# State products of a chunked scan in tiles of four heads instead of two, with a fourth output buffer and a new plan

## The chip, the cores and the metric

The kernel runs on one core of one Trainium2 chip. The metric is the device time of one execution in microseconds (us); lower is better. Before the change the median of three runs is 358.34 us (357.5 to 358.92).

## What is computed

A chunked state-space scan over `x` (4 batches, 8 heads, 768 steps, 32 channels, state size 16), whose result is the input of a gated feed-forward layer. All is float32. Cut to what matters:

```python
for c in range(nc):                       # the kernel uses chunks of 128 steps, in two halves of 64
    M = (C_c @ B_c.T) * L                 # L: decays between two steps, causal
    y_intra = M @ x_c
    y_inter = (C_c @ state) * exp(cum)    # what the state from before contributes
    y[c] = y_intra + y_inter
    state = decay_full * state + sum_j B_j x_j * decay_from_j     # 16 x 32 per head
x2 = y.transpose(0, 2, 1, 3).reshape(3072, 256)
out = (sigmoid(x2 @ w_gate) * (x2 @ w_val)) @ w_out               # 256 -> 1536 -> 256
```

## The kernel before, in words

The 768 steps are six chunks of 128 (`NCH`), and each chunk is two halves of 64 steps (`L2`). For each chunk the scan makes 512 token rows of the layer's input (four batches of 128), and the feed-forward part of chunk k (`gate`, `value`, `proj`) runs on the tensor engine (PE) while the scan of chunk k+1 is made. Chunk 0 has its own code (`FirstUnit`, one batch at a time); chunks 1 to 5 use class `Scan`. A float32 product that must keep full precision is either three products of float32r parts (L842, L871 to L873) or one plain f32 product (L518, L549, L564, L574, L867).

PE visits the scan of each chunk twice, between products of the feed-forward part. **Visit A** (`scan`) holds the products C·B (`multiply`, L549) and the halves' own state products (`own`, L574). **Visit B** (`weigh`) holds the weighted products (`within`, L564) and the products of C with the two states at the start of the two halves (L518). The states of the eight heads stand on 128 partitions, 16 rows a head.

`own` multiplies B (decayed, `bd`) by x for two heads at a time: a tile of 64 steps by 32 state rows (2 heads x 16) on PE, 64 columns of x (2 heads x 32) streamed through it. Half of what comes out belongs to the wrong head, so `chosen` (L582) multiplies it by a 0/1 mask on the vector engine (DVE). L518 uses such a state tile as weights, 32 rows by 64 columns, for 64 columns of C. Both make 32 products in a chunk (16 in `own` of chunk 5, which needs no state at its end), and each f32 product leaves two records in the trace.

The rest of the state: `early` (GpSimd, POOL) fades the old state by the decay of the first half (`sp`, L466), DVE adds the first half's own product (`sm`, L500), POOL fades that again (L466) and adds the second half's (L541) into `sn`.

The order of each engine is fixed in the program by a planner: every step has an engine, a cost, needs, and a due time (`DUES`); `VISIT_A` and `VISIT_B` are its costs for the two visits, `TURN` says behind which third of a projection visit B stands. PSUM gives the products three banks (`ps_mm`). Of the other functions the change touches, `proj` turns a projection by DVE transposes (L878) into `o` buffers, three in all, from which SyncE's queue (SP) writes the output (L885).

Of the kernel before, what the change touches and what calls it, by code (L numbers as in the profile page):

```python
# [44 lines left out]
}  # L45
WARM = (4, 4, 3)
# [12 lines left out]
POOL_SB = 1.32  # L59
# [15 lines left out]
VISIT_A, VISIT_B = 2.1, 2.68  # L75
HELD = 1
TURN = {2: 2, 3: 1, 4: 0, 5: 0}
# [8 lines left out]
def tile_ssd_then_gated_ffn(  # L86
# [21 lines left out]
    NG = H // NQ  # L108
    NK = DM // P
# [41 lines left out]
    nc.vector.tensor_reduce(of_h, eye.rearrange("p (h n) -> p h n", n=N), axis=mybir.AxisListType.X, op=ALU.add)  # L151
    of_g = const.tile([P, NG], F32, name="of_g")
# [7 lines left out]
    nc.gpsimd.tensor_copy(mask, of_g.rearrange("p (g o) -> p g o", o=1).broadcast_to([P, NG, D]))  # L160

# [46 lines left out]
    def run():  # L208
# [9 lines left out]
        spare = {"y": [0.0], "banks": [0.0] * 3, "cb": [0.0], "g": [0.0] * 3, "o": [0.0] * 3}  # L218
# [183 lines left out]
    def state_of(c, name, bufs):  # L402

        if (name, c) not in got:
            got[name, c] = wk.tile([P, NB, NG * D], F32, tag=name, name=f"{name}{c}", bufs=bufs)
        return got[name, c]
# [4 lines left out]
    class Scan:  # L411
# [51 lines left out]
        def faded(self, state, i):  # L463

            t = wk.tile([P, NB, NG * D], F32, tag="sp", name=f"sp{self.c}", bufs=1)
            nc.gpsimd.tensor_tensor(  # L466
                out=t, in0=state,
                in1=got["pp", self.c][:, :, i * L2 + L2 - 1 : (i + 1) * L2].broadcast_to([P, NB, NG * D]), op=ALU.mult,
            )
            return t  # L470

        def early(self):

            c = self.c
            yield step("pool", 0.7, [("S", c - 1)] + [("p", c, b) for b in range(NB)], [("sp", c)], port=True)
            self.sp = self.faded(states[c - 1], 0)

        def scan(self):

            c, more = self.c, self.more  # L480
            needs = [("mult", 0, b) for b in range(NB)] if c == 1 else []
            yield step(
                "pe", VISIT_A, [("bt", c), ("cg", c), ("xn", c), ("bdec", c)] + needs, [("cb", c)], cb=1, y=1, **({"banks": 1} if more else {})
            )
# [3 lines left out]
            pl = [pool.tile([P, NB, L2], F32, tag=tag, name=f"pl{c}") for pool, tag in ((ps_y, "py"), (ps_mm, "mm"))[: 1 + more]]  # L488
            for b in range(NB):
                own(self.bd[:, b], got["xn", c][:, b], lambda i, rows: pl[i][rows, b], b == 0, more)  # L490
            if more:
                yield step("dve", 0.42, [], [("after", c)], banks=-1)
                self.after = wk.tile([P, NB, NG * D], F32, tag="mr", name=f"mr{c}", bufs=1)
                chosen(self.after, pl[1], NB)
            yield step("dve", 0.42, y=-1)
            ml = wk.tile([P, NB, NG * D], F32, tag="ml", name=f"ml{c}", bufs=1)
            chosen(ml, pl[0], NB)
            yield step("dve", 0.42, [("sp", c)], [("first", c)], port=True)
            self.s1 = state_of(c, "sm", 1)
            nc.vector.tensor_tensor(out=self.s1, in0=self.sp, in1=ml, op=ALU.add)  # L500

        def weigh(self):
# [7 lines left out]
            yield step("pe", VISIT_B, [("mult", c), ("cd", c), ("first", c)] + ([("po", c - 1, 0, TURN[c])] if c > 1 else []), [("y", c), ("inter", c)])  # L510
# [58 lines left out]
    def own(bd, xn, out, first=False, more=True):  # L569

        for q in range(NQ):
            for i in range(2 if more else 1):
                half = slice(i * L2, (i + 1) * L2)
                nc.tensor.matmul(  # L574
                    out(i, slice(32 * q, 32 * q + 32)), bd[half, NG * q : NG * q + NG].rearrange("p g n -> p (g n)"),
                    xn[half, NG * q : NG * q + NG].rearrange("p g d -> p (g d)"),
                    start=first, stop=True, skip_group_check=True,
                )

    def chosen(out, local, n):  # L580

        nc.vector.tensor_tensor(  # L582
            out=out, in0=local,
            in1=mask.rearrange("p (o g) d -> p o (g d)", o=1).broadcast_to([P, n, NG * D]), op=ALU.mult,
        )

    class FirstUnit:
# [44 lines left out]
        def before(self):  # L632
# [3 lines left out]
            if ("cd", 0) not in got:  # L636
                got["cd", 0] = wk.tile([P, NB, L2], F32, tag="ml", name="cd0", bufs=1)
# [14 lines left out]
        def result(self):  # L652
# [35 lines left out]
            if ("mr", 0) not in got:  # L688
                got["mr", 0] = wk.tile([P, NB, NG * D], F32, tag="mr", name="mr0", bufs=1)
            self.after = got["mr", 0][:, b]  # L690
# [415 lines left out]
```

## Time and profile before

| | us |
|---|---|
| median of 3 runs | 358.34 |
| the profiled execution's own time | 358.31 |
| its span, first to last instruction | 356.2 |
| PE busy in it | 348.9 (98%) |
| DVE, ACT, POOL busy | 155.8, 134.2, 158.7 |

The profile is of one execution; 2.1 us of its time lie outside the span. "PEld" is the loading of weights into PE, which can overlap with its products; a wait is put down to what ended it. The chain of waits follows back from the last instruction to what released each step.

### The profile page before, as it was taken

The numbers are of one execution on the slowest core, as the hardware profiler recorded it, in microseconds if no ns is written. First come the engines' busy times: TensorE is split into PE (matmuls) and PEld (weight loads), VectorE is DVE, ScalarE is ACT, GpSimd is POOL, SyncE is SP. The second block draws the span as 40 slices with busy tenths as digits, with TensorE's granted clock in tenths as the row PEclk, the third lists the DMA queues.
The fourth block names the chain that finished last, engine by engine and source line by source line (L and its number), as shares of the span: only waits on it lengthen the run. The fifth ranks groups of instructions, "written<-read, shape, count | busy, mean of one in ns | idle before, by whom it ended". The sixth has DMA issues, their size and how long they took to land.

```text
span 356.2 us, 7756 instructions
## 1 busy us (share of the span) xinstructions
PE 348.9 (98%) x3174; PEld 269.8 (76%) x3174; DVE 155.8 (44%) x275; ACT 134.2 (38%) x241; POOL 158.7 (45%) x146
## 2 busy tenths in 40 slices
PE   8999999999999999999999999999999999999996
PEld 3674477457788888888888888888888888888885
DVE  6966677762474501655301655310655310232201
ACT  2667289242744401543410443320443320344400
POOL 4656377397698720357410357410365410244500
PEclk9999999999999999999999999999999999999999
DMA  6987999738644505445137321041200001200000
GB/s 130 194 249 249 265 210 216 133 65 60 99 93 90 81 19 72 89 93 72 32 44 137 50 46 25 29 63 25 33 4 2 1 4 25 33 4 0 1 31 29
DMA packets 96790, 27.57 MB, mean 77 GB/s; under 512 B 88370, under 2 KB 91442, under 8 KB 96114
## 3 DMA queue, kind: packets, MB, share of 16 engines
q1 hardware_dynamic: 96754, 27.07, 39.2%
q8 instruction: 25, 0.41, 0.5%
q14 instruction: 11, 0.09, 0.1%
HBM read 23.71 MB, written 3.34 MB: 76 GB/s over the span
## 4 chain that ended last, share of the span: by engine, by line
PE 81%; SPq 8%; DMA 7%; DVE 2%; issue 1%; DVEq 0%
PE pg L842 24%; PE pv L842 24%; PE po L871 6%; PE po L873 6%; PE po L872 6%; PE po L867 4%; DMA bq<-in_B_dram 3%; SPq L305 3%; PE po L908 2%; DMA wr<-in_moe_w_gate_dram 2%; SPq L342 2%; DMA wr<-in_moe_w_val_dram 2%; PE pcb L549 2%; PE pcb L564 2%; SPq L885 1%; PE pcb L518 1%
## 5 line engine op out<-in xcount | busy, mean ns | idle before, releaser
L801 POOL TENSOR_TENSOR h<-g,h 128x512 fp32r<-128x512 f32 x62 | 84.8, 1369 | 139.1 <-ACT h L799 139.1
L842 PE MATMUL pg<-xh,w 128*128 128x512 f32 x264 | 92.8, 392 | 1.3 <-DVE h L791 0.8
L842 PE MATMUL pv<-xh,w 128*128 128x512 f32 x264 | 92.1, 390 | 0.0
L795 DVE TENSOR_TENSOR g<-pv,g 128x512 f32<-128x512 f32 x62 | 42.8, 690 | 83.3 <-PE pv L842 82.9
L771 ACT ACTIVATE g<-pg 128x512 f32<-128x512 f32 x72 | 43.2, 600 | 68.6 <-PE pg L842 63.5
L799 ACT CAST h<-g 128x512 fp32r<-128x512 f32 x62 | 38.5, 620 | 78.8 <-DVE g L795 78.6
L842 PEld LDWEIGHTS pg<-xh,w 128*128 128x128 f32 x264 | 49.5, 188 | 13.4 <-DVE h L791 2.1
L842 PEld LDWEIGHTS pv<-xh,w 128*128 128x128 f32 x264 | 49.5, 188 | 10.6 <-POOL w L386 0.3
L842 PE MATMUL pg<-xl,w 128*128 128x512 f32 x132 | 51.4, 390 | 0.0
L842 PE MATMUL pv<-xl,w 128*128 128x512 f32 x132 | 51.4, 389 | 0.0
L871 PE MATMUL po<-h,w 128*128 128x512 f32 x100 | 40.2, 402 | 0.0
L873 PE MATMUL po<-h,w 128*128 128x512 f32 x100 | 39.0, 390 | 0.0
L872 PE MATMUL po<-h,w 128*128 128x512 f32 x100 | 38.9, 389 | 0.0
L842 PEld LDWEIGHTS pv<-xl,w 128*128 128x128 f32 x132 | 24.8, 188 | 5.2
L842 PEld LDWEIGHTS pg<-xl,w 128*128 128x128 f32 x132 | 24.8, 188 | 4.9
L878 DVE STREAM_TRANSPOSE o<-po 128x256 f32<-128x256 f32 x20 | 8.4, 448 | 45.9 <-PE po L873 30.8
L386 POOL TENSOR_TENSOR w<-wr,w 128x512 fp32r<-128x512 f32 x18 | 24.1, 1340 | 8.6 <-ACT w L384 6.9
L448 DVE TENSOR_TENSOR_SCAN ab<-ab,delta 128x512 f32<-128x512 f32 x20 | 24.9, 1260 | 3.1 <-DMA ab<-a_z 3.1
L369 POOL TENSOR_TENSOR wr<-wr 128x512 int32<-128x512 int32 x18 | 20.1, 1130 | 10.2 <-ACT wr L367 9.6
L871 PEld LDWEIGHTS po<-h,w 128*128 128x128 f32 x100 | 18.8, 188 | 4.4 <-issue 0.5
L872 PEld LDWEIGHTS po<-h,w 128*128 128x128 f32 x100 | 18.8, 188 | 4.2 <-issue 0.5
L873 PEld LDWEIGHTS po<-h,w 128*128 128x128 f32 x100 | 18.8, 188 | 4.0
(126 smaller groups left out, 377.9 us busy)
## 6 DMA issues: line engine op xcount, KB each, us to landing
ab<-a_z SPq DMA_DIRECT2D x10, 512.0 KB
wr<-in_moe_w_val_dram SPq DMA_DIRECT2D x6, 512.0 KB
wr<-in_moe_w_gate_dram SPq DMA_DIRECT2D x6, 512.0 KB
wr<-in_moe_w_out_dram SPq DMA_DIRECT2D x6, 512.0 KB
xn<-in_x_dram SPq DMA_DIRECT2D x5, 512.0 KB
out_dram<-o SPq DMA_DIRECT2D x160, 16.0 KB
bq<-in_B_dram SPq DMA_DIRECT2D x40, 32.0 KB
cq<-in_C_dram SPq DMA_DIRECT2D x40, 32.0 KB
```

Of the source, the lines that this page charges most:

```text
L369: nc.gpsimd.tensor_tensor(out=lw.bitcast(I32), in0=hw.bitcast(I32), in1=lw.bitcast(I32), op=ALU.add)
L386: engines[eng].tensor_tensor(out=lo, in0=lw, in1=hi.bitcast(F32), op=ALU.subtract)
L448: nc.vector.tensor_tensor_scan(out=t, data0=t, data1=delta.rearrange("p h l -> p (h l)"), initial=0.0, op0=ALU.mult, op1=ALU.add,)
L771: nc.scalar.activation(gs[k, f], pm, AF.Sigmoid)
L795: nc.vector.tensor_tensor(out=g, in0=pm, in1=g, op=ALU.mult)
L799: copies[eng](hh, g)
L801: engines[eng].tensor_tensor(out=hl, in0=g, in1=hh.bitcast(F32), op=ALU.subtract)
L842: nc.tensor.matmul(pm, w[:, part, kt, fs], xx[:, kt], start=(i == 0), stop=(i == 3 * NK - 1))
L867: nc.tensor.matmul(acc, whole[NF + f // 2][:, f % 2, ms], hs[k, f], start=start, stop=stop)
L871: nc.tensor.matmul(acc, hi, hh, start=start, stop=False)
L872: nc.tensor.matmul(acc, hi, hl, start=False, stop=False)
L873: nc.tensor.matmul(acc, lo, hh, start=False, stop=stop)
```

## The change

The state products of chunks 1 to 5 take four heads at once. `own` now gets tiles of 64 steps by 64 state rows, with 128 columns streamed; L518 (now L528) takes state tiles of 64 rows by 128 columns as weights. So each makes half as many products. The states of these chunks are twice as wide (four heads' columns, three quarters of them masked to zero by `wide_mask`). The order of the state's steps changes too: `early` fades straight into `sm` (L482), DVE adds the product unmasked (L505), DVE or POOL masks the sum (L507), and four DVE instructions fade and add (L552). The state that chunk 0 leaves is widened once on POOL (L474). There are four `o` buffers instead of three, two small tiles move to other buffers, the clock-warming products at the start are eleven of 128 columns instead of two of 512 and one of 384, and the plan (`DUES`, `VISIT_A`, `VISIT_B`, `TURN`) is new.

```diff
-WARM = (4, 4, 3)
+WARM = (1,) * 11
-VISIT_A, VISIT_B = 2.1, 2.68
+VISIT_A, VISIT_B = 1.95, 2.5
-TURN = {2: 2, 3: 1, 4: 0, 5: 0}
+TURN = {2: 2, 3: 1, 4: 3, 5: 0}
...
+    NW4 = H // 2
...
+    wide_mask = const.tile([P, NW4, D], F32, name="wide_mask")
...
         def early(self):
             c = self.c
-            yield step("pool", 0.7, [("S", c - 1)] + [("p", c, b) for b in range(NB)], [("sp", c)], port=True)
-            self.sp = self.faded(states[c - 1], 0)
+            if c == 1:
...
+            yield step("pool", 1.3, [("S", c - 1)] + [("p", c, b) for b in range(NB)], [("sp", c)], port=True)
+            self.s1 = state_of(c, "sm", 1)
+            nc.gpsimd.tensor_tensor(
+                out=self.s1, in0=states[c - 1],
+                in1=got["pp", c][:, :, L2 - 1 : L2].broadcast_to([P, NB, NW4 * D]), op=ALU.mult,
+            )
...
-                own(self.bd[:, b], got["xn", c][:, b], lambda i, rows: pl[i][rows, b], b == 0, more)
+                own(self.bd[:, b], got["xn", c][:, b], lambda i, rows: pl[i][rows, b], b == 0, more, NW4)
...
-                    for q in range(NQ):
-                        qs, rows = slice(32 * q, 32 * q + 32), slice(64 * (q % 2), 64 * (q % 2) + 64)
+                    for kt in range(NK):
+                        rows = slice(64 * kt, 64 * kt + 64)
                         nc.tensor.matmul(
-                            py[rows, i, q // 2, 0, b], state[qs, b], self.ct[qs, b, i * L2 : (i + 1) * L2],
+                            py[:, i, kt, 0, b], state[rows, b], self.ct[rows, b, i * L2 : (i + 1) * L2],
                             start=False, stop=True, skip_group_check=True,
                         )
...
-            yield step("pool", 0.7, [("first", c)], [], port=True)
-            sp = self.faded(self.s1, 1)
-            eng = yield step(("dve", "pool"), (0.42, 0.7), [("after", c)], [("S", c)], port=True)
-            states[c] = state_of(c, "sn", 2)
-            engines[eng].tensor_tensor(out=states[c], in0=sp, in1=self.after, op=ALU.add)
+            for b in range(NB):
+                yield step("dve", 0.31, [("after", c), ("first", c)], [("S", c)] if b == NB - 1 else [], port=True)
+                add_faded(states[c][:, b], self.s1[:, b], got["pp", c][:, b, L - 1 : L])
...
-            o = wk.tile([P, DM], F32, tag="o", name=f"o{k}_{m}{n}", bufs=3)
+            o = wk.tile([P, DM], F32, tag="o", name=f"o{k}_{m}{n}", bufs=4)
```

Three places show how the instructions stand. First PE at visit B of chunk 2, before; `sn` and `sm` are the states at the start of the two halves, `ct` is C, the size is that of the output:

```order
L873 MATMUL po_0_1488<-h_11_1504,w_894 128x512
L564 MATMUL pcb_1325<-ab_779,xn_1085 32x64 x64
L518 MATMUL pcb_1325<-ct_1138,sn_1048 64x64 x4
L518 MATMUL pcb_1325<-ct_1138,sm_1443 64x64 x4
L518 MATMUL pcb_1325<-ct_1138,sn_1048 64x64 x4
L518 MATMUL pcb_1325<-ct_1138,sm_1443 64x64 x4
```

and the same place in the changed kernel:

```order
L876 MATMUL po_0_1439<-h_11_1454,w_904 128x512
L575 MATMUL pcb_1294<-ab_793,xn_1081 32x64 x64
L528 MATMUL pcb_1294<-ct_1111,sn_911 128x64 x2
L528 MATMUL pcb_1294<-ct_1111,sm_1123 128x64 x2
L528 MATMUL pcb_1294<-ct_1111,sn_911 128x64 x2
L528 MATMUL pcb_1294<-ct_1111,sm_1123 128x64 x2
```

The visit keeps its place and its 64 weighted products; 32 state products became 16 that write all 128 partitions.

Second, DVE behind visit A of chunk 2, before (`mr`, `ml`: the masked own products; `ab`: the weighing of C·B; `g`: the gate times the value of the feed-forward part, which empties a PSUM bank):

```order
L795 TENSOR_TENSOR g1_8_1320<-pv1_8_1312,g1_8_1320 128x512
L582 TENSOR_TENSOR mr2_1409<-pl2_1359,mask_101 128x256
L582 TENSOR_TENSOR ml2_1414<-pl2_1358,mask_101 128x256
L553 TENSOR_TENSOR ab2_779<-pcb2_1325,ab2_779 128x512 x3
L500 TENSOR_TENSOR sm2_1443<-sp2_1117,ml2_1414 128x256
L553 TENSOR_TENSOR ab2_779<-pcb2_1325,ab2_779 128x512
L795 TENSOR_TENSOR g1_9_1427<-pv1_9_1418,g1_9_1427 128x512
```

and now:

```order
L798 TENSOR_TENSOR g1_8_1291<-pv1_8_1284,g1_8_1291 128x512
L594 TENSOR_TENSOR sn2_1359<-pl2_1328,wide_mask_113 128x512
L505 TENSOR_TENSOR sm2_1123<-sm2_1123,pl2_1327 128x512
L564 TENSOR_TENSOR ab2_793<-pcb2_1294,ab2_793 128x512 x4
L798 TENSOR_TENSOR g1_9_1374<-pv1_9_1367,g1_9_1374 128x512
L798 TENSOR_TENSOR g1_10_1404<-pv1_10_1397,g1_10_1404 128x512
L552 SCALAR_TENSOR_TENSOR sn2_1359<-sm2_1123,pp2_1057,sn2_1359 128x128
```

Two instructions of 512 elements stand where three of 256 stood, still ahead of the next `g`.

Third, SP's queue ahead of chunk 1 (`ab1`: the decays that are scanned for it; `pp1`: the products of decays), before:

```order
L346 DMA wr16_620<-in_moe_w_out_dram 128x2x512
L324 DMA ab1_674<-a_z_111 64x2048 x2
L330 DMA pp1_687<-a_p_112 128x1x128 x4
L324 DMA ab2_779<-a_z_111 64x2048 x2
L318 DMA bq2_785<-in_B_dram 128x1x64 x8
```

and now:

```order
L351 DMA wr16_632<-in_moe_w_out_dram 128x2x512
L329 DMA ab1_686<-a_z_123 64x2048
L335 DMA pp1_698<-a_p_124 128x1x128 x4
L329 DMA ab1_686<-a_z_123 64x2048
L329 DMA ab2_793<-a_z_123 64x2048 x2
L323 DMA bq2_799<-in_B_dram 128x1x64 x8
```

The second half of `ab1` moved behind the four transfers of `pp1`.

## Rows read from the trace of the kernel before

**Rows 1.** The page: span, PE's busy time, the granted clock by slices of 8.9 us (9 is full speed).

```profile
span 356.2 us, 7756 instructions
PE 348.9 (98%) x3174; PEld 269.8 (76%) x3174; DVE 155.8 (44%) x275; ACT 134.2 (38%) x241; POOL 158.7 (45%) x146
...
PEclk9999999999999999999999999999999999999999
```

**Rows 2.** Busy time of each engine in two stretches in the middle (us from the span's start, length, then PE, PEld, DVE, ACT, POOL with their counts, the clock, DMA share, GB/s).

```profile
100.00:150.00 50.00, 50.00 (x521) 41.23 (x520) 21.91 (x37) 16.62 (x28) 24.33 (x20) 1.00 0.46 77
200.00:300.00 100.00, 100.00 (x1009) 82.40 (x1008) 40.17 (x69) 33.05 (x55) 39.08 (x31) 1.00 0.14 23
```

**Rows 3.** The waits of PE: who waited for whom, us in total, times, longest.

```profile
PE warm L140 <- DVE warm_sb L137: 1.1, 1, 1.1
PE pg L842 <- DVE h L791: 0.8, 1, 0.8
PE pg L842 <- DVE o L878: 0.4, 1, 0.4
```

**Rows 4.** The chain of waits at the visits of chunks 1, 2 and 5 and some products beside them (start, us, what, records; a few records are missing from the counts).

```profile
62.89 10.30 PE po L867 x24
73.19 1.14 PE pcb L549 x63
...
112.81 1.14 PE pcb L549 x62
113.95 0.79 PE pl L574 x53
114.74 1.58 PE pg L842 x6
116.32 1.36 PE pv L842 x6
...
131.28 1.41 PE pcb L564 x91
132.69 1.09 PE pcb L518 x64
...
272.75 0.58 PE pl L574 x32
```

**Rows 5.** The loads of weights, grouped by line and shape (tile rows*columns, weights, count, busy us, mean ns of one).

```profile
L842 PEld LDWEIGHTS pg<-xh,w 128*128 128x128 f32 x264 | 49.5, 188 | 13.4 <-DVE h L791 2.1 <-PE pv L842 0.8
L518 PEld LDWEIGHTS pcb<-ct,sm 32*64 32x64 f32 x160 | 4.2, 133 | 0.0
L574 PEld LDWEIGHTS pl<-xn,bd 64*32 64x32 f32 x288 | 3.3, 105 | 0.9 <-issue 0.7 <-POOL wr L369 0.2
L732 PEld LDWEIGHTS pp<-apb,of_row 32*128 32x128 f32 x2 | 0.3, 182 | 0.2 <-POOL bd L648 0.2
```

**Rows 6.** The timeline of PEld (start, us from the first start to the last end, records): two stretches of L678, visit A of chunk 2, and the first and the last of the eight groups of eight of L518 in visit B of chunk 2.

```profile
13.50 0.53 PEld L678 LDWEIGHTS mm<-cd,wide 128*128 128x128 f32 x4
24.03 0.53 PEld L678 LDWEIGHTS mm<-cd,wide 128*128 128x128 f32 x4
112.74 0.96 PEld L549 LDWEIGHTS pcb<-cg,bt 32*64 32x64 f32 x64 [0.35 <-issue]
...
132.62 0.21 PEld L518 LDWEIGHTS pcb<-ct,sn 32*64 32x64 f32 x8
...
133.43 0.21 PEld L518 LDWEIGHTS pcb<-ct,sm 32*64 32x64 f32 x8
```

**Rows 7.** The chain of waits just ahead of chunk 1's first product.

```profile
88.34 1.52 DMA out_dram<-o
90.18 0.46 DVE o L878
90.77 1.62 PE pg L842 x6
```

**Rows 8.** The timeline of DVE behind visit A of chunk 2 (start, us, line, what, count).

```profile
115.02 0.42 DVE L582 TENSOR_TENSOR mr<-pl,mask 128x256 f32<-128x256 f32 x1 [1.40 <-PE pl L574]
115.36 0.41 DVE L582 TENSOR_TENSOR ml<-pl,mask 128x256 f32<-128x256 f32 x1
115.69 1.88 DVE L553 TENSOR_TENSOR ab<-pcb,ab 128x512 f32<-128x512 f32 x3
117.48 0.41 DVE L500 TENSOR_TENSOR sm<-sp,ml 128x256 f32<-128x256 f32 x1
118.42 0.68 DVE L795 TENSOR_TENSOR g<-pv,g 128x512 f32<-128x512 f32 x1
```

**Rows 9.** Chunk 1 in the timeline: SP's issues, the scan on DVE, POOL, and visit B on PE.

```profile
54.16 1.15 SPq L324 DMA_DIRECT2D ab<-a_z  x2
55.36 3.07 SPq L330 DMA_DIRECT2D pp<-a_p  x4
64.45 4.57 DVE L448 TENSOR_TENSOR_SCAN ab<-ab,delta 128x512 f32<-128x512 f32 x4 [3.07 <-DMA ab<-a_z]
69.16 1.10 POOL L453 TENSOR_TENSOR bd<-bn,ab 128x512 f32<-128x512 f32 x1 [5.32 <-DVE ab L448]
78.48 1.27 POOL L461 TENSOR_TENSOR ct<-ct,pp 128x512 f32<-128x512 f32 x1
81.78 1.48 PE L564 MATMUL pcb<-ab,xn 64*32 64x64 f32 x128
```

More of the change, by code (lines that the diff above doesn't have):

```diff
@@ L461, in before @@
             engines[eng].tensor_tensor(out=self.ct, in0=self.ct, in1=got["pp", c], op=ALU.mult)
[L463 to L470, printed above, removed]
         def early(self):
             c = self.c
-            yield step("pool", 0.7, [("S", c - 1)] + [("p", c, b) for b in range(NB)], [("sp", c)], port=True)
-            self.sp = self.faded(states[c - 1], 0)
+            if c == 1:
+                yield step("none", 0.0, [("S", 0)])
+                narrow, states[0] = states[0], wk.tile([P, NB, NW4 * D], F32, tag="sn", name="sw0", bufs=2)
+                nc.gpsimd.tensor_tensor(
+                    out=states[0].rearrange("p b (o d) -> p b o d", o=2),
+                    in0=narrow.rearrange("p b (o d) -> p b o d", o=1).broadcast_to([P, NB, 2, NG * D]),
+                    in1=wide_mask.rearrange("p (x o g) d -> p x o (g d)", x=1, o=2).broadcast_to([P, NB, 2, NG * D]),
+                    op=ALU.mult,
+                )
+            yield step("pool", 1.3, [("S", c - 1)] + [("p", c, b) for b in range(NB)], [("sp", c)], port=True)
+            self.s1 = state_of(c, "sm", 1)
+            nc.gpsimd.tensor_tensor(
+                out=self.s1, in0=states[c - 1],
+                in1=got["pp", c][:, :, L2 - 1 : L2].broadcast_to([P, NB, NW4 * D]), op=ALU.mult,
+            )
         def scan(self):
@@ L487, in scan @@
                 multiply(self.pcb[:, :, b * L : (b + 1) * L], self.bt[:, b], self.cg[:, b])
-            pl = [pool.tile([P, NB, L2], F32, tag=tag, name=f"pl{c}") for pool, tag in ((ps_y, "py"), (ps_mm, "mm"))[: 1 + more]]
+            pl = [pool.tile([P, NB, NW4 * D], F32, tag=tag, name=f"pl{c}") for pool, tag in ((ps_y, "py"), (ps_mm, "mm"))[: 1 + more]]
             for b in range(NB):
-                own(self.bd[:, b], got["xn", c][:, b], lambda i, rows: pl[i][rows, b], b == 0, more)
+                own(self.bd[:, b], got["xn", c][:, b], lambda i, rows: pl[i][rows, b], b == 0, more, NW4)
             if more:
[L492 to L500, printed above, removed]
+                yield step("dve", DVE_MM, [], [("after", c)], banks=-1)
+                states[c] = state_of(c, "sn", 2)
+                chosen(states[c], pl[1], NB, wide_mask, NW4)
+            yield step("dve", DVE_MM, [("sp", c)], y=-1)
+            nc.vector.tensor_tensor(out=self.s1, in0=self.s1, in1=pl[0], op=ALU.add)
+            eng = yield step(("dve", "pool"), (DVE_SB, POOL_SB), [], [("first", c)], port=True)
+            engines[eng].tensor_tensor(
+                out=self.s1, in0=self.s1,
+                in1=wide_mask.rearrange("p (o g) d -> p o (g d)", o=1).broadcast_to([P, NB, NW4 * D]), op=ALU.mult,
+            )
         def weigh(self):
@@ L536, in state, with add_faded @@
             c = self.c
-            yield step("pool", 0.7, [("first", c)], [], port=True)
-            sp = self.faded(self.s1, 1)
-            eng = yield step(("dve", "pool"), (0.42, 0.7), [("after", c)], [("S", c)], port=True)
-            states[c] = state_of(c, "sn", 2)
-            engines[eng].tensor_tensor(out=states[c], in0=sp, in1=self.after, op=ALU.add)
+            for b in range(NB):
+                yield step("dve", 0.31, [("after", c), ("first", c)], [("S", c)] if b == NB - 1 else [], port=True)
+                add_faded(states[c][:, b], self.s1[:, b], got["pp", c][:, b, L - 1 : L])
+    def add_faded(new, old, by):
+        nc.vector.scalar_tensor_tensor(out=new, in0=old, scalar=by, in1=new, op0=ALU.mult, op1=ALU.add)
     def multiply(out, bt, cg):
@@ L567, in within, with own @@
                     )
-    def own(bd, xn, out, first=False, more=True):
-        for q in range(NQ):
+    def own(bd, xn, out, first=False, more=True, g=NG):
+        for q in range(H // g):
+            heads = slice(g * q, g * q + g)
             for i in range(2 if more else 1):
@@ L574, in own, with chosen @@
                 nc.tensor.matmul(
-                    out(i, slice(32 * q, 32 * q + 32)), bd[half, NG * q : NG * q + NG].rearrange("p g n -> p (g n)"),
-                    xn[half, NG * q : NG * q + NG].rearrange("p g d -> p (g d)"),
-                    start=first, stop=True, skip_group_check=True,
-                )
[L580 to L585, printed above, removed]
+                    out(i, slice(16 * g * q, 16 * g * (q + 1))), bd[half, heads].rearrange("p g n -> p (g n)"),
+                    xn[half, heads].rearrange("p g d -> p (g d)"), start=first, stop=True, skip_group_check=True,
+                )
+    def chosen(out, local, n, m=mask, g=NG):
+        m = m.rearrange("p (o g) d -> p o (g d)", o=1)
+        nc.vector.tensor_tensor(out=out, in0=local, in1=m.broadcast_to([P, n, g * D]), op=ALU.mult)
     class FirstUnit:
@@ L687, in result @@
             yield step("dve", 0.21, [], [("after", 0, b)], banks=-1)
-            if ("mr", 0) not in got:
-                got["mr", 0] = wk.tile([P, NB, NG * D], F32, tag="mr", name="mr0", bufs=1)
-            self.after = got["mr", 0][:, b]
-            chosen(self.after.rearrange("p (o c) -> p o c", o=1), py[1][:, NK:], 1)
+            states[0] = state_of(0, "sn", 2)
+            chosen(states[0][:, b : b + 1], py[1][:, NK:], 1)
         def take(self, i):
@@ L707, in state @@
             yield step("dve", 0.24, [("after", 0, b), ("first", 0, b), ("p0",)], [("S0", b)] + [("S", 0)] * (b == NB - 1), port=True)
-            states[0] = state_of(0, "sn", 2)
-            nc.vector.scalar_tensor_tensor(
-                out=states[0][:, b], in0=self.s1, scalar=got["p0"][:, b, L2 - 1 : L2], in1=self.after, op0=ALU.mult, op1=ALU.add
-            )
+            add_faded(states[0][:, b], self.s1, got["p0"][:, b, L2 - 1 : L2])
     def first_products():
@@ L718, in first_products @@
         yield step("dve", 0.28)
-        ap0 = const.tile([R2, L2], F32, name="ap0")
+        ap0 = hp.tile([R2, L2], F32, tag="h1", name="ap0")
         nc.vector.tensor_tensor_scan(
@@ L735, in first_products @@
         yield step("act", 0.38, [], [("p0",)], banks=-1)
-        got["p0"] = hp.tile([P, NB, L2], F32, tag="h5", name="pp0")
+        both = hp.tile([P, 2, NB, L2], F32, tag="h5", name="pp0")
+        got["p0"], got["cd", 0] = both[:, 0], both[:, 1]
         nc.scalar.copy(got["p0"].rearrange("p b l -> p (b l)"), pp[:, : NB * L2])
@@ L918, in last_proj @@
         yield step("act", ACT_HALF, [], [], o=1)
-        o = wk.tile([P, DM], F32, tag="o", name=f"o{k}_{j}", bufs=3)
+        o = wk.tile([P, DM], F32, tag="o", name=f"o{k}_{j}", bufs=4)
         nc.scalar.copy(o, acc[:, :DM])
@@ L941, in tile_ssd_then_gated_ffn @@
     nc.scalar.activation(table, table, AF.Sigmoid)
-    ac = const.tile([R2, L2], F32, name="ac")
+    ac = hp.tile([R2, L2], F32, tag="h11", name="ac")
     nc.vector.tensor_scalar(out=ac, in0=a0, scalar1=1e-6, scalar2=1.0, op0=ALU.max, op1=ALU.min)
```

11 lines of the change are left out of this document (6 added, 5 removed), and 52 rows, old and new, of the table DUES.

## The prediction

> **What bounds the kernel now.** I read the page first: PE is busy for 348.9 of 356.2 us, at the full clock of 2.4 GHz in every slice [rows 1]. Then the windows: between 100 and 150 us and between 200 and 300 us PE is busy without any gap, while DVE and POOL work less than half of the time [rows 2]. Then PE's waits: the longest is 1.1 us, and all of them together are some 4 us, all before 91 us [rows 3]. So the kernel is PE's list of work, one item behind the other. A change pays or costs what it does to that list, and the other engines matter only where they would make PE wait. So the question is how long the new state products hold PE, ten times: once in each visit A and each visit B of chunks 1 to 5. The chain gives the old prices: the own products (L574) take 0.79 us in a visit, 0.58 in chunk 5 with half as many, and the products with the states (L518) take 1.09 [rows 4].
>
> The sum is made against the profiled execution, 358.31 us (356.2 of span and 2.1 around it); the median of the runs, 358.34, is the same number.
>
> **What a small product costs.** An f32 product leaves two records, and each streams its columns twice: 24 records of 512 columns take 10.30 us, 0.429 each [rows 4], which is 1,024 columns at 2.4 GHz. So a record of 64 columns holds its tile for 0.054 us and one of 128 for 0.107. Tiles on different rows or columns of PE run beside each other. L549 shows both: 64 records of 128 columns on eight tiles, eight behind each other on a tile, need 1.14 us in all [rows 4], and 8 x 0.107 is 0.86 of that.
>
> The loading of weights has a price of its own, set by the columns of the weights and not by their rows: one load takes 105 ns at 32 columns, 133 at 64, 188 at 128, and still 182 at 128 columns on only 32 rows [rows 5]. Most of that is pipeline; what counts is how fast loads follow each other. L678 loads 128 columns for only 64 streamed ones, and its four loads take 0.53 us in both stretches: less the last one's 0.19, that is three steps of 0.113 us, twice the 0.054 that the streaming needs [rows 6]. There PE waits for weights. In L518 the eight groups of eight start between 132.62 and 133.43, so eight records need 0.116 us, and each of the four row quarters takes a record every 0.058 us [rows 6]. A 64-column load at L678's rate would need 0.056 and the streaming needs 0.054: before the change the two are just in balance.
>
> **Visit A, own products.** Removed: 32 products on eight tiles (64 records, eight behind each other on a tile, 64 columns: 8 x 0.054 = 0.43 us; the other 0.36 of the 0.79 is start, end and issue). Added: 16 products on four tiles, again eight records behind each other on a tile, but of 128 columns: 8 x 0.107 = 0.86. Halving the instructions halves what is not the bound; the columns that a tile has to stream double. Chunk 5 before shows the overhead with half the instructions: 0.58 - 0.43 = 0.15. So the new time is 1.00 at least, and at most L549's 1.14, which has eight such records per tile and twice the products. I take 1.05, nearer to the row with few instructions: +0.26 in four visits. In chunk 5 the eight products fall on two tiles, still eight records each: 1.00 against 0.58, +0.42. Sum +1.5 us (bounds +1.3 and +1.9).
>
> **Visit B, products with the states.** Removed: 64 records on four row quarters, 16 behind each other at 0.058 (0.93 of the 1.09; 0.16 around it). Added: 32 records on two row halves, again 16 behind each other, each with 64 columns streamed but 128 columns of weights. No row shows a tile of 64 rows by 128 columns. Nearest below is the streaming alone: 16 x 0.054 + 0.16 = 1.02. Nearest in shape is L678, with the same weights' columns and the same streamed columns: 0.113 a record, 16 x 0.113 + 0.16 = 1.97. The highest end is that the halves do not load beside each other: 32 x 0.113 + 0.16 = 3.78. I take 1.97, since L678 differs only in its rows, which the load does not feel [rows 5], and since row groups do load beside each other in L518. That is +0.88 in each of five visits, +4.4 us (bounds -0.35 and +13.4).
>
> The Trainium skill speaks against this overlap: its page "TensorE: Matmul & The Clock Gate", section "The mechanism" in Part 3, says that a weight load overlaps with a running matmul only when the row groups differ. In L549 each row quarter holds two tiles that stream 0.107 us a record, and eight records per tile fit into 0.96 us of loads [rows 6], about 0.11 each, so the load must lie beside the streaming of its own rows; by the rule it would be 0.16 and the stage 1.3 us. The trace does not bear the rule out.
>
> **The fourth output buffer.** Before chunk 1's first product the chain runs from an output transfer to a DVE transpose at 90.18 to PE at 90.77 [rows 7]; PE waits 0.4 us there [rows 3], and its first six products take 1.62 instead of 1.36. With four buffers no transpose of chunk 0 waits for an output of chunk 0. Gain 0.4 to 0.66; I take 0.5. What is late next is PE itself.
>
> **DVE and POOL.** Behind visit A of chunk 2, DVE needs 3.40 us from the first mask (115.02) to the next `g` (118.42) [rows 8]. Now two instructions of 512 elements and four weighings stand there, some 0.6 apart as the three weighings are: 3.6. The bank of `g`'s value is wanted by the second gate after it, 114.74 + 1.58 + 3 x 1.36 = 120.4, and `g` is read by 119.3: nothing is lost; without that 1.1 us of cover the 0.2 would show on PE. POOL gets two instructions of about 1.3 a chunk (as L461 in [rows 9]) for three of 0.6 to 0.7, on an engine that idles over half of the time: nothing. The prologue gets one more small reduction and one more small copy while PE still runs its clock-warming products, of as many columns as before: nothing. The three waits between 37 and 54 us hang on when weights land behind other transfers; the longest is 0.8 [rows 3], its queue is nearly as before, so I take no change, with 0.8 either way.
>
> **Chunk 1.** The second half of `ab1` is issued behind `pp1`, 3.07 us later [rows 9]. The scan, now started at 64.45, needs both, and `bd` behind it ends at 70.26; visit A starts at 73.19 [rows 4], so 2.9 us cover it. On POOL the early fade and the mask must then be done by visit B at 81.78: from 70.26 eight instructions of 1.1 to 1.3 (as L453 and L461) stand there, to about 80.3. If all 3.07 arrive, visit B waits up to 1.5 us. I take 0: transfers shared the engines before too.
>
> **Sum.** 358.31 + 1.5 + 4.4 - 0.5 = **363.7 us**, 1.5% slower.
>
> **Rivals.**
> - *Streaming is the bound in visit B, not the loads.* For it: in L518 load and streaming cost the same, so the row cannot tell which one bound it. Against it: L678, and 182 ns for 128 columns on 32 rows. Visit B then takes 1.02: 358.31 + 1.5 - 0.35 - 0.5 = 359.0, no change that can be measured.
> - *Faster: the number of instructions decides.* For it: 0.36 of the 0.79 in visit A is not streaming. If time follows records at the old price, the ten stages halve: 4 x 0.40 + 0.29 + 5 x 0.55 = 4.6 saved, 353.3 with the output buffer; at L564's 1.41 / 128 = 0.011 a record [rows 4] it is 354.5. I write 354. It decides only as long as a tile's eight records stream in less time than all records of the stage take to issue, so up to 0.79 us of streaming for the old count. Against it: with four tiles the streaming alone is 0.86 us. The Trainium skill has a rule for this side, in "TensorE: Matmul & The Clock Gate", section "Wait — 56ns, not 53.3ns?": starts never come closer than about 25 ns, however few the columns. By it 304 fewer records would save 7.6 us; 64 records in 0.79 us are 12 ns apart, so the trace contradicts it for tiles.
> - *A load waits for its own half's product* and starts when that has streamed: 16 x (0.113 + 0.054) + 0.16 = 2.83 in visit B, 1.74 more each, +8.7: 368.0. Against it stands L549's pace above. It is what the section "The mechanism" of that page of the Trainium skill would make of this tile.
> - *The two halves load one behind the other*: 3.78, +13.4: 372.7. L518's four quarters speak against it.
>
> **How the numbers follow.** Forecast 0.62, streaming 0.16, instructions 0.12, own half's product 0.06, one behind the other 0.04. About 0.5% (1.8 us) is what a measurement can tell from no change: faster is below 356.5, slower above 360.1. Faster is the instructions' 0.12, same the streaming's 0.16, slower the rest, 0.72. The range leaves out the instructions and the halves one behind the other (0.16 together) and takes in the streaming rival less 0.7 of the waits before 91 us, and the own half's product: 358.3 to 368.3.
>
> **What would show it.** In the profile after: L528 at 1.9 to 2.0 us in the chain, its loads 0.11 us apart in pairs; the new own products at 1.0 to 1.1, in chunk 5 no shorter than in the others; no DVE wait for an output transfer near 90 us; PE without gaps from 100 us on. Wrong, if L528 takes 1.1 us or less, if PE waits for DVE or POOL at a visit, or if the stretch before 91 us moves by over 1 us.

## The result: 362.06 us, slower by 1.1%

The changed kernel takes 362.06 us, median of six runs (361.84 to 362.8), against 358.44 for six runs of before beside it: ratio 1.0108, interval 1.0092 to 1.0125. The forecast was 363.7 within 358.3 to 368.3, the direction "slower". The profiled execution took 362.8 us and is the slowest of the six; its span is 361.0, so 1.8 us lie outside it. Its mean granted clock is 0.995; the other five executions list 1.000.

### The profile after

First the page of the changed kernel, answering to [rows 1]: busy time, the granted clock in 40 slices, and one DMA queue that matters further down.

```profile
PE 355.0 (98%) x2886; PEld 279.6 (77%) x2886; DVE 160.9 (45%) x288; ACT 132.9 (37%) x240; POOL 161.3 (45%) x145
...
PEclk9989999999999999999999999999999999999999
...
q8 instruction: 22, 0.36, 0.4%
```

PE has 288 records fewer (304 in the visits, while the warm-up has 16 more) and is busy for 6 us longer. It is still the bound. The clock dips in the third slice, behind the longest of its waits, answering to [rows 3]:

```profile
PE py L195 <- DVE sm L594: 1.5, 1, 1.5
PE warm L141 <- DVE warm_sb L138: 1.1, 1, 1.1
PE pa L608 <- DVE ab L611: 0.2, 1, 0.2
```

No wait at a visit, and none behind the first 22 us: the waits for `h`, `o` and the rest between 37 and 91 us are gone. The wait for `sm` at 22 us is 1.5 us long; before it was 0.4. The chain at visit A of chunk 2, visit B of chunk 2 and visit A of chunk 5 (start, us, what), answering to [rows 4]:

```profile
113.11 1.14 PE pcb L560 x61
114.25 1.03 PE pl L586 x32
...
134.55 1.41 PE pcb L575 x91
135.97 1.93 PE pcb L528 x32
...
276.33 1.02 PE pl L586 x16
```

The own products take 1.03 us where they took 0.79, in chunk 5 1.02 with half the records, where they took 0.58; the products with the states 1.93 where they took 1.09. The weight loads of the latter, by form, answering to [rows 5] (mean ns of one is the last number ahead of the second bar):

```profile
L528 PEld LDWEIGHTS pcb<-ct,sm 64*128 64x128 f32 x80 | 6.1, 188 | 0.0
L586 PEld LDWEIGHTS pl<-xn,bd 64*64 64x64 f32 x144 | 4.3, 132 | 0.9 <-issue 0.9
```

and their timeline in visit B of chunk 2, the first two and the last of eight groups, answering to [rows 6]:

```profile
135.89 0.30 PEld L528 LDWEIGHTS pcb<-ct,sn 64*128 64x128 f32 x4
136.11 0.31 PEld L528 LDWEIGHTS pcb<-ct,sm 64*128 64x128 f32 x4
...
137.45 0.31 PEld L528 LDWEIGHTS pcb<-ct,sm 64*128 64x128 f32 x4
```

From the first group to the last are seven steps in 1.56 us, 0.223 a group of four: on each of the two row halves a record every 0.111 us, L678's rate. Last DVE behind visit A of chunk 2, answering to [rows 8]:

```profile
115.35 0.69 DVE L594 TENSOR_TENSOR sn<-pl,wide_mask 128x512 f32<-128x512 f32 x1 [1.44 <-PE pl L586]
115.96 0.68 DVE L505 TENSOR_TENSOR sm<-sm,pl 128x512 f32<-128x512 f32 x1
116.55 2.48 DVE L564 TENSOR_TENSOR ab<-pcb,ab 128x512 f32<-128x512 f32 x4
118.95 0.68 DVE L798 TENSOR_TENSOR g<-pv,g 128x512 f32<-128x512 f32 x1
```

From the mask to the next `g` are 3.60 us, and PE does not wait for it.

### Where the time went

Stage by stage along PE, both executions counted from their first instruction: the dense feed-forward of chunk 0 starts 1.36 us later (25.89 after 24.53) and is 1.64 shorter, up to its projections (36.56 after 38.20); the visits A cost 4 x 0.24 + 0.44 = 1.40 more, the visits B 5 x 0.84 = 4.20; the feed-forward from chunk 1's first product to visit A of chunk 2 is 0.52 shorter (24.73 after 25.25). That makes +4.80, the difference of the spans; 0.3 less lies outside the span.

The wait of 1.5 us is only 0.21 of the 1.36: PE had come to it earlier than before and goes on at 22.06 instead of 21.85. The other 1.15 us lie behind it, where the granted clock fell. Two stages of six equal products there, and the window of 10 us around them in the changed kernel and in before:

```profile
22.06 0.94 PE py L195 x6
...
23.77 1.58 PE mm L195 x6
...
20.00:30.00 10.00, 8.47 (x83) 7.23 (x84) 6.72 (x16) 5.63 (x13) 5.59 (x5) 0.83 0.96 319
20.00:30.00 10.00, 9.60 (x106) 7.08 (x105) 7.69 (x18) 7.34 (x16) 6.44 (x7) 1.00 0.86 283
```

The number behind the five engines is the granted clock. Six products that take 0.94 us at 2.4 GHz take 1.58 in the stretch that is largely at 1.2 GHz.

### The profile page after: what moved, and what is told of

It reads as the page before. It is cut to its first block, busy times and chain, and to the rows that moved or that the text cites. A ratio compares the mean times of both kernels' runs of the same rounds, so it can differ in the third digit from the quotient of the medians.

```text
span 361.0 us, 7221 instructions
## 1 busy us (share of the span) xinstructions
PE 355.0 (98%) x2886; PEld 279.6 (77%) x2886; DVE 160.9 (45%) x288; ACT 132.9 (37%) x240; POOL 161.3 (45%) x145
## 3 DMA queue, kind: packets, MB, share of 16 engines
HBM read 23.71 MB, written 3.34 MB: 75 GB/s over the span
## 4 chain that ended last, share of the span: by engine, by line
PE 93%; SPq 4%; DMA 2%; DVE 0%; issue 0%; ACT 0%
PE pg L845 25%; PE pv L845 25%; PE po L874 7%; PE po L875 6%; PE po L876 6%; PE po L870 5%; PE pcb L528 3%; SPq L310 2%; PE pv L836 2%; PE pg L836 2%; PE po L911 2%; PE pcb L575 2%; PE pcb L560 2%; DMA wr<-in_moe_w_val_dram 2%; PE pl L586 1%; PE po L912 1%
## 5 line engine op out<-in xcount | busy, mean ns | idle before, releaser
L804 POOL TENSOR_TENSOR h<-g,h 128x512 fp32r<-128x512 f32 x62 | 83.2, 1342 | 115.1 <-ACT h L802 115.0
L453 DVE TENSOR_TENSOR_SCAN ab<-ab,delta 128x512 f32<-128x512 f32 x20 | 24.0, 1214 | 6.4 <-DMA ab<-a_z 6.4
L539 ACT CAST xh<-pcb 128x512 fp32r<-128x512 f32 x10 | 5.9, 586 | 45.0 <-PE pcb L528 41.1
L874 PEld LDWEIGHTS po<-h,w 128*128 128x128 f32 x100 | 18.8, 188 | 4.4 <-issue 0.5
L875 PEld LDWEIGHTS po<-h,w 128*128 128x128 f32 x100 | 18.8, 188 | 4.2 <-issue 0.5
```

What stands on the lines that cost most here:

```text
L453: nc.vector.tensor_tensor_scan(out=t, data0=t, data1=delta.rearrange("p h l -> p (h l)"), initial=0.0, op0=ALU.mult, op1=ALU.add,)
L804: engines[eng].tensor_tensor(out=hl, in0=g, in1=hh.bitcast(F32), op=ALU.subtract)
L874: nc.tensor.matmul(acc, hi, hh, start=start, stop=False)
L875: nc.tensor.matmul(acc, hi, hl, start=False, stop=False)
```

## Experiments on the tiles

### Streaming twice under the same loads

```diff
+                        cols = self.ct[rows, b, i * L2 : (i + 1) * L2].rearrange("p (o l) -> p o l", o=1)
...
-                            py[:, i, kt, 0, b], state[rows, b], self.ct[rows, b, i * L2 : (i + 1) * L2],
+                            py[:, i, kt, :, b], state[rows, b], cols.broadcast_to([64, 2, L2]),
```

> The changed kernel, but each product of visit B streams its 64 columns of C twice (128 columns, the second copy goes to a part of the PSUM bank that nothing reads any more); loads, tiles and their number stay. If the load of 128 columns of weights is the bound (0.112 a record), the 0.107 of the doubled streaming lies beside it and visit B stays at 1.93 to 2.0. If streaming were the bound, or if a load waited for its own half's product, it would grow by 16 x 0.054 = 0.86 to 2.8 or more in each visit, 4.3 us in all.

Measured: 362.81 us in one run. The chain at visit B of chunk 2:

```profile
134.37 1.41 PE pcb L576 x91
135.78 1.99 PE pcb L529 x32
```

1.99 after 1.93. Twice the streamed columns fit under the same loads, so loads set visit B's time, and products of a half run beside the next load of the same half: the rivals "streaming is the bound" and "a load waits for its own half's product" fall.

### Own products with half the streamed columns

```diff
-                own(self.bd[:, b], got["xn", c][:, b], lambda i, rows: pl[i][rows, b], b == 0, more, NW4)
+                own_half(self.bd[:, b], got["xn", c][:, b], lambda i, rows: pl[i][rows, b, :64], b == 0, more)
...
+                    xn[half, 4 * q : 4 * q + 2].rearrange("p g d -> p (g d)"), start=first, stop=True, skip_group_check=True,
```

> The changed kernel, but each own product of visit A streams only the first two of its four heads (64 columns instead of 128); its 16 products and four tiles stay, and DVE reads the 64 columns twice. This leaves out half of the own products. If the columns that a tile streams decide (8 x 0.107 + 0.17 = 1.03 measured), eight records of 64 columns take 8 x 0.058 and visit A's own products 0.6 to 0.7 us, in chunk 5 as well; the time falls by 0.35 to 0.4 in each of five visits, near 360.2. If the 64 by 64 tile or the number of records decides, they stay at 1.03.

Measured: 361.18 us in one run. The chain at visit B of chunk 1 and at visit A of chunk 2:

```profile
80.58 1.36 PE pcb L582 x88
81.94 1.11 issue
83.06 0.31 PE pcb L582 x6
...
114.23 0.62 PE pl L593 x32
```

With the same number of records the own products take 0.62 us instead of 1.03: the streamed columns of a tile decide, not the number of instructions. That was the rival on the other side. The weighted products of chunk 1, which nothing touched, took 2.78 us instead of 1.41, with PE stopped for 1.11 us for nothing the profile shows. These 1.4 us more cover the 1.0 by which the time lies above the 360.2 expected.

### Quarters again, and half columns, in visit B

```diff
-                    for kt in range(NK):
-                        rows = slice(64 * kt, 64 * kt + 64)
+                    for q in range(NQ):
+                        qs, cols = slice(32 * q, 32 * q + 32), slice(64 * (q % 2), 64 * (q % 2) + 64)
...
-                            py[:, i, kt, 0, b], state[rows, b], self.ct[rows, b, i * L2 : (i + 1) * L2],
+                            py[cols, i, q // 2, 0, b], state[qs, b, cols], self.ct[qs, b, i * L2 : (i + 1) * L2],
```

> The changed kernel with one thing undone: the products with the states (visit B) again take row quarters, 32 rows by 64 columns of the wide state, 32 of them a visit; the wide states, the wide own products, the plan and the buffers stay, and every other engine's list is the same. If the loading of 128-column weights is what visit B pays for (1.93 us after, 1.09 before), it goes back to 1.09 in each of five visits and the time falls by 4.2 us, from 362.1 to 357.9. If the cost comes from the wide states or the new plan around it, visit B stays at 1.9 and the time at 362.

Measured: 362.89 us (362.39 to 363.86), ratio 1.0139 (1.0095 to 1.0184). In chunks 1, 2 and 5 the products take the 1.09 us expected; in chunks 3 and 4 they take 2.93. The other form, 64 rows by 64 columns of weights:

```diff
+                        for j in range(2):
+                            cols = slice(64 * j, 64 * j + 64)
...
+                                py[cols, i, kt, 0, b], state[rows, b, cols], self.ct[rows, b, i * L2 : (i + 1) * L2],
...
```

> The changed kernel, but each product of visit B with a state tile of 64 rows by 128 columns is cut into two of 64 rows by 64 columns, on four tiles of the array: 32 products, 64 records, 16 behind each other on a tile. If a load costs by its columns, and tiles load beside each other, a record takes 0.058 us and visit B 1.09. If two tiles on the same rows load one after the other, 16 x 2 x 0.058 + 0.16 = 2.0. If the number of products decides, 64 records instead of 32 make it longer than 1.93.

Measured: 366.79 us in one run; 1.09 us in chunks 1, 2 and 5, 3.32 and 3.39 in chunks 3 and 4. Its time is 3.9 above the kernel with quarters: besides the longer stops, the granted clock was 0.61 for 3 us behind the first of them, and PE waits 0.9 us for `xh` in chunk 1. So the price of the tile is as forecast, and set by the columns of its weights and not by its rows: 64 rows by 64 columns cost what 32 by 64 did. But of the 4.2 us that the quarters should give back, the stops in chunks 3 and 4 took 3.7 (twice 2.93 less 1.09). The 0.5 that is left fits the profiled executions, whose span is 360.6 after 361.0. What stopped these products is the question of a later section.

## Experiments on the plan and the buffers

Before with four output buffers (`bufs=3` to `bufs=4` in `proj`); before with the new `DUES`, `WARM`, `VISIT_A`, `VISIT_B`, `TURN`; before with both; and the changed kernel with three buffers. The planner counts the buffers too, so that a buffer more or less also moves steps: visit A of chunk 2 stands 24 products later in before with four, and 12 later in the changed kernel with three.

> The kernel before with a fourth output buffer alone. The wait ahead of chunk 1's first product (0.4 us on PE, 0.26 more in the first six products) should go: 0.4 to 0.66 us less, about 357.9. If something else holds that product (a bank, SP's queue), no change.

Measured: 357.46 us (356.61 to 359.38), ratio 0.9979 (0.996 to 0.9998): slightly faster, the only kernel here below before. Its profile has no wait for an output transfer, but its span is before's 356.2, because the waits for `h` and `sm` are longer in that execution (1.8 and 1.2 us).

> The kernel before with the plan of the changed one alone: its due times, its eleven clock-warming products, its costs of the visits and its places of visit B; tiles, states and three output buffers as before. The changed kernel lost 5.6 us in the visits but only 3.6 in all, so 2 us came back elsewhere: 0.5 of it ahead of chunk 1, and some 1.6 as waits of PE in chunk 0's feed-forward part that are gone. If the plan took those away, this kernel is 1.0 to 1.6 us faster than before, near 357. If they went for another reason (a later start of PE, other landings), it stays at 358.4.

Measured: 361.25 us (360.18 to 362.9), ratio 1.009 (1.0063 to 1.0117), a miss by 4 us. L518 takes 1.09 us in four visits and 3.34 in chunk 4.

> The kernel before with both: the new plan and four output buffers, but the old tiles. It is what the change leaves when its tiles are taken out: 362.1 - 5.6 = 356.5 if the two parts are independent, and the fastest of all. If the plan needs the wide states to pay, 358.

Measured: 361.97 us (359.52 to 363.39), ratio 1.0092 (1.0059 to 1.0125), a miss by 5.5 us. L518 takes 3.13 in chunk 4. Two windows behind that visit (us, PE busy and count, PEld, DVE, ACT, POOL; then the granted clock):

```profile
246.30:249.00 2.70, 2.70 (x14) 2.09 (x9) 1.23 (x2) 1.18 (x2) 0.00 (x0) 0.60 1.47 180
249.00:252.00 3.00, 3.00 (x12) 2.38 (x12) 0.15 (x1) 0.00 (x0) 0.00 (x0) 0.79 0.23 30
```

The stop of 2 us is followed by a stretch largely at 1.2 GHz: the 24 projection records behind the visit take 7.17 us, where the changed kernel has 5.58. Stop and low clock are 3.6 us together; the rest of the miss stays open.

> The changed kernel with three output buffers again. If the fourth buffer is worth what the wait ahead of chunk 1 took, 0.4 to 0.66 us, this is 362.6; if the new plan has moved the transposes clear of the transfers, no change.

Measured: 363.28 us (362.17 to 364.74), ratio 1.014 (1.0115 to 1.0165), 1.2 above the changed kernel. Its profile shows no wait for an output transfer, so this run does not say where the difference lies, and the fourth buffer need not be what took that wait out of the changed kernel's profile.

Then the changed kernel with before's plan:

```diff
-VISIT_A, VISIT_B = 1.95, 2.5
+VISIT_A, VISIT_B = 2.1, 2.68
-TURN = {2: 2, 3: 1, 4: 3, 5: 0}
+TURN = {2: 2, 3: 1, 4: 0, 5: 0}
...
```

> The changed kernel (its tiles, four output buffers) with the plan of before: due times, warm-up, costs and places of the visits. What the visits cost stays: L528 1.93 us in chunks 1 to 5, own products 1.03 us. Theory, the new plan took TensorE's waits of 37 to 54 us away (and made one of 1.5 us at 21 us) and so paid for 1.6 us of the visits: with the old plan the sum of the prediction comes out, 358.3 + 1.4 + 4.2 - 0.5 = 363.4 us (362.8 to 364.2), with waits for h and o near 37, 44 and 54 us. Rival, the plan is worth nothing or costs something (before with the new plan measured 361.25 us, and without its one stop of 2.25 us some 359.0, 0.6 over before): 361.5 to 362.1 us. By the theory of blocks no visit stops.

Measured: 366.62 us (366.2 to 367.05), ratio 1.0222 (1.0198 to 1.0246), 3.2 us more than my account gave. The visits cost what was expected. The chain in chunk 1, behind visit B:

```profile
86.59 1.96 PE pcb L528 x32
...
88.57 0.59 ACT xh L539
...
91.28 2.50 PE pg L845 x5
93.78 1.84 PE pv L845 x6
```

and the windows there:

```profile
88.00:91.00 3.00, 0.97 (x11) 0.57 (x9) 1.90 (x5) 2.23 (x4) 1.21 (x1) 1.00 0.16 22
91.00:93.50 2.50, 2.28 (x6) 1.82 (x6) 0.23 (x1) 0.06 (x1) 1.38 (x2) 0.55 0.22 33
```

The wait for `h` near 44 us did come back (1.2 us, balanced by a start 0.9 earlier). But with the old due times all of chunk 0's projections stand ahead of visit B of chunk 1, so nothing lies between that visit and the products that need its result: PE waits 2.0 us for `xh`, and then stands largely at 1.2 GHz, which costs 2.0 more. On the new tiles the new plan is worth 4.5 us, most of it this place and not the three waits I had named.

## What stopped the small products

In the five kernels with such an unexplained length, seven visits had one gap of 1.3 to 2.2 us from one record to the next in the middle of a run of small products (five kernels, not four, as the expectation below has it). Here is the chain in visit B of chunk 4 of the kernel with quarters:

```profile
243.82 1.41 PE pcb L575 x91
245.24 0.61 PE pcb L528 x29
245.85 1.53 issue
247.37 0.79 PE pcb L528 x35
```

PE waits for nothing that another engine does. Counting all records of PE, of PEld and of PE's sequencer (semaphores and drains) from the start, 4,545 stand ahead of this stop; ahead of the others stand 3,521 (twice), 4,545 again, 4,801 (twice) and 1,473. All leave 193 when divided by 256. The DMA view of 244.5 to 245.0 us in that kernel has one instruction packet:

```profile
GB/s 82 31 82 11 21 10 10 0 0 0 0 0 0 0 0 0 0 0 0 0 1311 0 0 0 0 0 72 51 72 72 72 123 92 123 124 72 113 41 82 21
...
q8 instruction: 1, 0.02, 14.8%
```

It begins in the slice of 244.75 us, 0.8 us behind record 4,289 (256 ahead of the stop), and PE goes on 2.6 us after it; over the seven stops that is 2.3 to 2.9 us. The whole run has 24 such packets of 16 KB for its 6,127 records: 255 records a packet. My reading is that PE gets its instructions in blocks of 256, and that a block that is over in 1.7 us can be over before the next has come. The Trainium skill, page "Runtime: NRT & Kernel Launch", section "Instruction fetch mechanics", says the same of the blocks (16 KiB, 256 instructions) but calls the cost mostly hidden behind the issue of instructions; with L575's 128 loads and 128 products in 1.41 us, 5.5 ns each, it is not.

Where blocks begin can be shifted without touching anything else. Three kernels got 25 to 29 tiny products in the warm-up, in place of 256 columns of its own products; here the edit of the kernel before:

```diff
-WARM = (4, 4, 3)
+WARM = (4, 4, 1)
...
+    for k in range(25):
+        cols = slice(32 * (k % 4), 32 * (k % 4) + 32)
+        nc.tensor.matmul(warm[cols, :64], warm_sb[:64, cols], warm_sb[:64, :64], start=True, stop=True, skip_group_check=True)
```

> The kernel before with 25 tiny products added to the warm-up (tiles of 64 by 32, the last warm-up product shorter for it, so that the warm-up takes as long): 100 TensorE records more, and the order of everything else on all engines as before. In four traces the runs of small products stopped for 1.3 to 2.2 us, seven times, and each time exactly at a record whose number on TensorE leaves 193 when divided by 256; an instruction packet of 16 KB (256 records of 64 bytes) began 0.4 to 1.3 us after the last record with that remainder. Theory, instructions come in blocks of 256: a visit B of before has 384 records in 2.5 us, and where such a record falls among its first 130, a whole block is over in 1.7 us, before the next one has come. In before it falls 159 to 212 records into the visits of chunks 2 to 5; 100 records more put it at 112, 86, 59 and 72, so all four visits should stop for 1.7 to 2.2 us inside L518's products (now L521), at their records 369, 343, 316 and 329 of 384: 358.4 + 7.4 = 365.8 us (363 to 367). Rival, the stops come with the new plan (its transfers or its clock): none here, 358.4 us.

Measured: 369.31 us (366.97 to 372.3), ratio 1.0305 (1.0234 to 1.0377), above the 363 to 367 expected: 25 tiny products slow the kernel before by 11 us. The profiled execution is the one of 369.31. The chain at the five stops (chunks 1 to 5), each with the rest of L521 behind it:

```profile
83.12 3.60 issue
86.73 0.35 PE pcb L521 x9
...
137.40 1.37 issue
138.77 0.34 PE pcb L521 x8
...
189.97 1.40 issue
191.37 0.57 PE pcb L521 x21
...
242.57 1.73 issue
244.30 0.79 PE pcb L521 x35
...
298.36 1.64 issue
300.00 0.68 PE pcb L521 x28
```

In chunks 2 to 5 the 8, 21, 35 and 28 products' records left, of 64 with as many loads, are the places forecast (records 369, 343, 316 and 329 of 384). A fifth stop, in chunk 1, was not forecast, because I had counted that visit from a semaphore instruction 4 us ahead of its products; from the first product the block begins 111 records in, and it is over in 1.71 us like the others. Its packet began 2.2 us behind the block's first record, later than at any other stop, and PE went on 3.3 us after that. Behind this stop the granted clock was 0.53 for 3 us. L521's five visits take 16.6 us together instead of 5.45, which is 11.1 more; what the low clock adds (1.7), the waits up to 91 us that this execution does not have take off again.

> The changed kernel with the same shift: 27 tiny products for two of the warm-up's eleven, 100 TensorE records more, everything else in its order. Theory of blocks: visit B now has 320 records, and its last 64 take 1.93 us, so that a block that begins in it lasts 3.8 us or more wherever it begins; the remainder falls 141, 251, 121, 150 and 76 records into the visits of chunks 1 to 5. No stop, 362.1 us (361.5 to 363.2: chunk 2's block begins 5 records ahead of the visit and is over in 2.3 us, which may stop it for up to 1.1 us). Rival, any kernel of this size stops somewhere when it is shifted: 364 us or more.

Measured: 362.4 us (361.78 to 362.61), ratio 1.0101 (1.0072 to 1.013). No stop; L528 1.93 us in all five visits.

> The first of these experiments (the changed kernel with the quarters in visit B, which measured 362.9 us with stops of 1.80 and 1.74 us in chunks 3 and 4) with 29 tiny products for two of the warm-up's eleven: 108 records more, everything else in its order. Theory of blocks: the remainder moves from 31, 93, 58 and 176 records into the visits of chunks 2 to 5 to 179, 241, 206 and 68. The stops of chunks 3 and 4 go, and one comes in chunk 5, at record 325 of 384, for 1.7 to 2.2 us: 362.9 - 3.5 + 1.9 = 361.3 us (360.5 to 362). Rival, the stops belong to chunks 3 and 4 (their transfers, their place in the plan): they stay, 362.9 us.

Measured: 360.71 us (359.42 to 362.33), ratio 1.0065 (1.0042 to 1.0089), 2.2 below the same kernel unshifted. The chain in chunks 4 and 5:

```profile
243.90 1.09 PE pcb L531 x64
...
289.81 0.72 PE pcb L531 x34
290.53 1.18 issue
291.71 0.69 PE pcb L531 x30
```

The stops of chunks 3 and 4 are gone and one stands in chunk 5, with 30 products' records left (record 325 of 384: 60 are left with their loads). So the stops belong to the numbering, not to a chunk or the plan. Where visit B's tiles have 64 columns of weights, all twelve stops came where a block began 57 to 112 records into the visit, and none where it was 137 or more; in before it is 159 to 212. From a block's first record to the next block's it was 3.0 to 3.9 us at these stops, and 5.5 at the long one. In the changed kernel the 64 records of 1.93 us stretch a block that begins inside the visit to 4.2 us or more (4.2 in the shifted one, 6.2 and more as it stands). Blocks that begin a few records ahead of it are shorter (2.66 us in chunk 1, 2.20 in chunk 4) and did not stop, since the next packet had begun before them; but the same block of chunk 1 is the one that stopped the kernel with half of the own products. So it is out of the way of most of this, not immune.

With that the new plan on before's tiles can be read: 361.25 less the one stop of 2.25 us is by estimate 359.0, 0.6 above before and not 1.4 below. Still open: why three blocks that were over as fast did not stop PE, those of 1.54 us in chunk 2 of the kernels with quarters and with half columns, and one of 1.58 us in chunk 1 of the changed kernel with before's plan. In all three the next packet began ahead of the block, by 1.3 to 3.1 us; what lets one begin early, no run tells.

## Why the prediction came out as it did

- **PE's list of work is the bound**: right. PE is busy 98%, and nothing behind 22 us waits.
- **Visit A**: forecast 1.05 and +1.5 in all; measured 1.03 and +1.40. The reason holds as well: with the same records and half the columns it is 0.62.
- **Visit B**: forecast 1.97 and +4.4; measured 1.93 and +4.20. Loads at L678's rate (0.111 us), beside the streaming (1.99 when it is doubled), the two row halves beside each other.
- **Fourth buffer**: forecast -0.5; the stretch that holds the wait is 0.52 shorter, so the size is right. That the buffer is the reason is not shown here: the changed kernel with three buffers does not wait there either. In before the buffer alone takes 0.2% off, and with it the planner's order changes. One reading was wrong without harm: chunk 1's first product starts at 87.50 us in before, and the wait at 90.77 [rows 7] stands ahead of its thirteenth.
- **DVE and POOL**: forecast 3.6 us on DVE and no wait; measured 3.60 and none. Chunk 1's visit B does not wait either.
- **The waits up to 54 us**, taken as no change within 0.8, are the term that was mis-sized, in both directions: -1.64 where the three waits of 37 to 54 us went, +1.36 where PE waits for `sm` at 22 us and then has the low clock. Their sum hides them, and that is luck: visit A of chunk 1 starts at 72.84 instead of 73.12. Neither follows from the plan. The shifted kernel with the changed kernel's order waits 0.4 us at 22 us, and its profiled execution is 1.0 shorter; the shifted kernel with before's plan has no wait for `h`, and its dense feed-forward takes 36.63 us, as short as the changed kernel's; three kernels with the new plan (streaming twice, half of the own products, quarters shifted) wait 0.9 us for `h`. What sets these waits in an execution stays open.
- **Rivals**: the 353.3 of the rival that counts instructions should be 353.2; nothing hangs on it.

The profiled execution thus gives 358.31 + 1.40 + 4.20 - 0.52 + 1.36 - 1.64 - 0.3 = 362.8. Against the forecast of 363.7, the visits give 0.3 of the difference, the early waits 0.3, the time outside the span 0.3. The median lies 0.7 lower still: the other five executions list a granted clock of 1.000, so that the 1.15 us of low clock at 24 us should be missing in them; they have no trace to show it.

What the prediction did not see is that before's 1.09 us has a condition: it holds only where no block of instructions begins in the wrong place. A rival "the new numbering stops a visit" was missing, worth 2 us and more for each visit hit. That the changed kernel has no stop was not foreseen; one or two would still have been inside the range.

## What to carry to other kernels

Price a small tile by the slower of two rates, the columns that it streams and the columns of weights that its row group loads; both were within 4% here, from rows of other products. Where 256 small records follow each other in 3 us or less (the stops here came behind blocks of 1.6 to 1.7 us, and one behind 2.9), count where the blocks of 256 begin before a difference of 1% is put down to an edit: shift the numbering with a few idle products and measure again. Plan and tiles belong together: the old due times cost 4.5 us on the new tiles.

## What was not expected of the hardware

- PE can stop where a block of 256 records ends: for 1.4 to 3.8 us where the block was over in 1.7 us (twelve times in six kernels), and for 1.3 us behind a block of 2.9 us in the kernel with half of the own products. Three blocks of 1.5 to 1.6 us did not stop it.
- After such a stop the granted clock sometimes falls to the 1.2 GHz level for about 3 us (0.60 in before with plan and buffers, 0.61 behind the first of the kernel with half columns, 0.53 behind the longest of the shifted kernel) and sometimes stays at 1.00 (behind the other four of the shifted kernel).
- 25 idle products at the start of a kernel cost 11 us of 358.
